# Two x blocks and the second-stage weights as float32 through the ScalarE and SyncE queues, in a convolution and spectral-mixing kernel

## The chip, the cores and the metric

The kernel runs on one core of a Trainium2 chip. The time is the device time of one execution in microseconds (us). The engines are TensorE (PE; its weight loads are PEld in the profile), VectorE (DVE), ScalarE (ACT), GpSimd (POOL) and SyncE (SP). Transfers can be issued from the queues of POOL, SP and ACT; the core has 16 DMA engines that serve them all.

## The reference

Two stages follow each other. The inputs are float32.

```python
# x: (8, 3264, 192), weight: (8 heads, 7 taps)
w = softmax(weight, axis=-1)
# causal convolution of 7 taps along the sequence; head h has channels 24*h .. 24*h+23
c[b, s, h, :] = sum_k w[h, k] * x_padded[b, s + k, h, :]      # 6 zero rows in front

X = rfft(c, axis=1)[:, :64]                                   # 64 modes, w_r and w_i: (64, 192, 192)
Yr = X.real @ w_r - X.imag @ w_i                              # per mode
Yi = X.real @ w_i + X.imag @ w_r
u = c + irfft(Yr + 1j*Yi, n=3264, axis=1)                     # all other modes are zero
out = u + relu(u @ w_ch)                                      # w_ch: (192, 192)
```

## The kernel before

**Data.** The whole of x is kept on chip as bf16 in `xall`. A sequence of 3264 rows is cut into two halves of 1632 rows, each of six blocks of 256 rows and a rest of 96 rows. Sequences go in pairs `q` (four of them). One "block half" is a block `b` of one half `h` for both sequences of a pair: 128 partitions times two runs of 384 elements. There are 48 of them; the list `halves` has them in the order in which they are wanted, the last pair and the last block first. `load_halves(n)` (L188) issues the next n on POOL's queue, whose transfers turn float32 into bf16 on the way. `load_rest` (L199) issues the four transfers of the rests.

**Order of the work.** The schedule is manual: each engine runs its instructions in the order in which the program issues them. At the start

- SP loads `weight` into `wraw`, copied to 128 partitions (a source list of `[14, 4], [0, 32], [1, 14]`);
- POOL issues one block half, writes three index tables (`cidx`, `sidx`, `midx`, L212 to L216), then issues nine more halves, the rests and the other halves, with a few small constants (`ident`, `order`, `perm`) between;
- VectorE and ScalarE make the softmax of the taps and from it the band matrices of the convolution (`band`; masks from `cidx` L228, softmax L232 to L248, taps put in place L253, copies of the band L256 to L264). VectorE then makes the phases of the Fourier tables from `sidx` and `midx` (L265 to L269), of which ScalarE takes the sines (`table(0)`, L277 to L279); VectorE clears some entries of that table (L282).

**Convolution and Fourier sums.** PE first does `rows_ahead` (L338), which needs the first two block halves and whose result ScalarE copies (L343), and then 24 filler matmuls (L524). Then come six units of two parts each, with eight heads in a unit; one head is 16 matmuls (L385) into one of four pairs of PSUM banks, which VectorE or ScalarE empties (L399, L401). The first unit reads ten block halves: eight of its own, and for the rows before them the two of the next block, which the matmuls with partitions 64 to 127 read a little later. VectorE adds and subtracts the halves (L419), PE makes the Fourier sums (`dft`, L436), and transposes (L493) fill in between.

**Mode weights.** `load_w` (L319) loads the weights of the modes in 16 groups on POOL's queue, after x and after the second-stage weights. PE multiplies them from L590 on, with the last transposes between. Some groups wait until a buffer is free (`wnext`).

**Second stage.** `wa` holds rows 0 to 127 of `w_ch`, `wb` the rows 128 to 191 twice, and `wc` (made from `wa` by ScalarE, L921) the two halves of `wa` swapped. They are needed from the mode stage on. The products are on L737, the clamp is on L783, the sum on L805 and the stores on SP's queue behind it.

The lines of the loads at the start that the change touches:

Of the kernel before, what the change touches and what calls it, by code (L numbers as in the profile page):

```python
# [12 lines left out]
F32 = mybir.dt.float32  # L13
BF16 = mybir.dt.bfloat16
# [5 lines left out]
def kernel(  # L20
# [9 lines left out]
    nc = tc.nc  # L30
    B, S, D = x.shape
# [8 lines left out]
    P = 128  # L40
    NQ = B // 2
    HS = S // 2
# [19 lines left out]
    def sb(name, shape, dtype):  # L62
        return pool.tile([P] + shape, dtype, tag=name, name=name)
# [8 lines left out]
    xall = sb("xall", [NQ, TQ, 2, D], BF16)  # L72
# [5 lines left out]
    mixa = sb("mixa", [3 * 2 * B * MODES], BF16)  # L78
    xt = mixa[:, :].rearrange("p (j k m) -> p j k m", j=3, k=2 * B)
    zw, zy = [mixa[:, B * D * t:B * D * (t + 1)].rearrange("p (b d) -> p b d", b=B) for t in range(2)]  # L80
    wa = sb("wa", [D], BF16)
    wb = sb("wb", [D], BF16)
    wc = sb("wc", [D], BF16)
    ident = sb("ident", [P], BF16)
    ascale = sb("ascale", [1], F32)
# [8 lines left out]
    spare = sb("spare", [NK - 4, 2 * D], F32)  # L94
# [13 lines left out]
    ctw = [ct[:, q, :, :, :].rearrange("p k t c -> p (k t c)") for q in range(NQ)]  # L108
# [76 lines left out]

    halves = [(q, b, h) for q in range(NQ)[::-1] for b in range(NBH)[::-1] for h in range(2)]

    def load_halves(n):  # L188
        for _ in range(n):
            q, b, h = halves.pop(0)  # L190
            k = 2 + 4 * b + 2 * h
            src = bass.AP(tensor=x.tensor, offset=x.offset + (2 * q * S + HS * h + 2 * P * b) * D,
                          ap=[[2 * D, P], [S * D, 2], [1, 2 * D]])
            nc.gpsimd.dma_start(out=xall[:, q, k:k + 2, :, :].rearrange("p k t d -> p k (t d)"), in_=src)  # L194


    R0 = (P - RR) // 2
# [1 line left out]
    def load_rest():  # L199
        for i in range(2):  # L200
            for h in range(2):
                src = bass.AP(tensor=x.tensor, offset=x.offset + (i * S + HS * (2 - h) - RR) * D,
                              ap=[[2 * D, RR // 2], [2 * S * D, NQ], [1, 2 * D]])
                nc.gpsimd.dma_start(out=xall[64 * h + R0:64 * h + 64, :, i, :, :].rearrange("p q t d -> p q (t d)"),
                                    in_=src)
# [2 lines left out]
    wr3 = wraw.rearrange("p (h k) -> p h k", h=G4)  # L208
    nc.sync.dma_start(out=wraw, in_=bass.AP(tensor=weight.tensor, offset=weight.offset,
                                            ap=[[G4 * KK, 4], [0, 32], [1, G4 * KK]]))  # L210
    load_halves(1)
    nc.gpsimd.iota(cidx, pattern=[[1, PW]], base=0, channel_multiplier=-1, allow_small_or_imprecise_dtypes=True)  # L212
    nc.gpsimd.iota(sidx.rearrange("p (b a) -> p b a", a=2), pattern=[[2 * P, NBH + 1], [1, 2]], base=0,
                   channel_multiplier=2, allow_small_or_imprecise_dtypes=True)
    nc.gpsimd.iota(midx.rearrange("p (r j) -> p r j", r=2), pattern=[[1, 2], [2, JH]], base=0,
                   channel_multiplier=0, allow_small_or_imprecise_dtypes=True)  # L216
    load_halves(9)
    load_rest()
    nc.vector.memset(packed, 0.0)
    nc.scalar.copy(out=bd3[:, :, PW:2 * PB], in_=packed[:, 0:1].unsqueeze(2).to_broadcast([P, H, 2 * PB - PW]))  # L220
# [13 lines left out]
                            in1=wmax.unsqueeze(2).to_broadcast([P, G4, KK]), op=ALU.subtract)  # L234
    nc.scalar.activation(out=wexp, in_=wsub, func=ACT.Exp)
    nc.scalar.activation(out=sgn[:], in_=halfpi[:], func=ACT.Sin)

    for h in range(2):
        rest = sidx[64 * h:64 * h + 64, 2 * NBH:NTF]
# [11 lines left out]
    for k in range(KK):  # L251
        e, v = divmod(KK - 1 - k, 2)
# [3 lines left out]
    for g in range(4):  # L256
        for r in range(4):
            c0 = 32 * (r % 2)
            dst = bd4[32 * r:32 * r + 32, G4 * g:G4 * (g + 1), :, c0:c0 + PW]
            srcv = pk4[32 * g:32 * g + 32, :, :, :]  # L260
            if r == 3 or (r == 2 and g > 1):
                nc.scalar.copy(out=dst, in_=srcv)
            else:
                nc.vector.tensor_copy(out=dst, in_=srcv)  # L264
    nc.vector.tensor_tensor(out=kp3, in0=sidx.unsqueeze(2).to_broadcast([P, NTF, MODES]),  # L265
                            in1=midx.unsqueeze(1).to_broadcast([P, NTF, MODES]), op=ALU.mult)
    nc.vector.tensor_scalar(out=turns, in0=kprod, scalar1=MAGIC, scalar2=None, op0=ALU.add)
# [20 lines left out]
    def select(dst, fill, base, pattern):  # L288
        nc.gpsimd.affine_select(out=dst, in_=dst, compare_op=ALU.not_equal, fill=fill, base=base,
                                pattern=pattern, channel_multiplier=1)  # L290

    load_halves(4)
    nc.gpsimd.memset(ident[:], 0.0)
    load_halves(2)
# [11 lines left out]
        load_halves(2)  # L306
        select(pv, 1.0 if c else -1.0, -JH * (1 - c), [[-1, JH], [-2 * JH, 2]])
    load_halves(len(halves))
    nc.gpsimd.dma_start(out=wa[:, :], in_=moe_w_ch[0:P, :])
    for i in range(2):  # L310
        nc.gpsimd.dma_start(out=wb[64 * i:64 * i + 64, :], in_=moe_w_ch[P:D, :])


    NG = MODES // 4
# [205 lines left out]

    rows_ahead(NQ - 1)

    for _ in range(24):
        nc.tensor.matmul(cz[3][64:P, 0, 0:2 * D], ahead[64:P, :], xall[64:P, NQ - 1, 2 + 4 * (NBH - 1), :, :].rearrange(  # L524
            "p t d -> p (t d)"), start=True, stop=True, tile_position=(64, 64), skip_group_check=True)
    prev = []
# [2 lines left out]
    for k, u in enumerate(units):  # L529
# [5 lines left out]
        for h in range(H):  # L535
            conv_head(u, h, "v" if h in ((0, 1, 3, 5) if k == 0 else (0, 4)) else "a")
            if h in (1, 5) and prev:
                q, b0, nb, rest = prev.pop(0)
# [383 lines left out]
    for g, beside in enumerate((0, 1, 1, 1, 2, 2, 2, 2, 2, 2, 2, 2, 2, 2, 0, 0)):  # L922
        d = g // 2
# [64 lines left out]
```

## Time and profile before

| | |
|---|---|
| median of 3 runs | 173.25 us (172.99 to 174.1) |
| profiled execution | 172.99 us |
| its span, from the first to the last instruction | 171.1 us |
| busy: PE, DVE, ACT, POOL | 92%, 73%, 72%, 38% of the span |
| POOL's queue | 23088 packets, 19.96 MB written |
| read from HBM, written to HBM | 39.43 MB, 20.45 MB |

The page divides the span into 40 equal slices; a digit is the busy share of an engine in tenths. In the rows of the timeline and of the groups stand the start in us, the duration in us, the engine, the line, the operation, out<-in with partitions x elements, and in brackets the idle time of the engine just before and what ended it. A list of waits has: who waited for whom, us in total, how often, the longest. In the view by stretches ("windows") each row has the stretch, its length, then the busy time and the number of instructions of PE, PEld, DVE, ACT and POOL, the granted TensorE clock, the mean load of the DMA engines (over 1 where packets overlap) and GB/s. In the view of DMA, a queue's row has packets, MB and the time its packets took as a share of 16 engines; the GB/s line has 40 slices of the stretch asked for; an issue's row has the number of transfers, KB of each, and us from issue to landing.

### The profile page before, as it was taken

Reading aid. Unit: us, or ns where it says so; the run is one execution under the profiler, and the core shown is the slowest. Engines: PE = TensorE matmul, PEld = TensorE weight load, DVE = VectorE, ACT = ScalarE, POOL = GpSimd, SP = SyncE. Lnnn points to the kernel's source line nnn. Section 1 sums busy time; section 2 is a strip of 40 time slices with the busy share of each in tenths; the row PEclk is TensorE's granted clock in tenths of the full one; section 3 lists DMA queues with packets and bytes.
Section 4 is the critical chain, followed back from the end, with each engine's and each line's share of the span. In section 5 each row is a group of like instructions: output and inputs, shape, how many; then the busy total and the mean of one; then the engine's idle time right before and its main releaser. Section 6 shows DMA issues by size and latency. Waiting matters only on the chain.

```text
span 171.1 us, 6152 instructions
## 1 busy us (share of the span) xinstructions
PE 157.1 (92%) x2599; PEld 118.9 (69%) x2599; DVE 125.3 (73%) x242; ACT 122.6 (72%) x224; POOL 64.4 (38%) x108
## 2 busy tenths in 40 slices
PE   0499999899999999998999999999999999999970
PEld 0255676566766666776776775888999989999930
DVE  3991857876493999944456562699989999899980
ACT  6656377858597688376685672779889899888840
POOL 7967999676766754434334002500000000000000
PEclk9999999999999999999999999999999999999995
DMA  2999999999999999999999993499969999899994
GB/s 28 162 183 200 201 201 204 198 201 201 203 204 194 201 209 203 206 206 206 206 207 207 206 179 71 108 387 340 322 244 390 371 361 374 318 357 377 353 382 144
DMA packets 38335, 40.71 MB, mean 238 GB/s; under 512 B 3652, under 2 KB 38212, under 8 KB 38308
## 3 DMA queue, kind: packets, MB, share of 16 engines
q0 software_dynamic: 23088, 19.96, 73.0%
q1 hardware_dynamic: 14948, 20.16, 32.7%
q8 instruction: 20, 0.33, 0.7%
q10 hardware_dynamic: 272, 0.20, 0.3%
q14 instruction: 7, 0.06, 0.1%
HBM read 39.43 MB, written 20.45 MB: 350 GB/s over the span
## 4 chain that ended last, share of the span: by engine, by line
PE 50%; DMA 34%; POOL 9%; issue 2%; DVE 1%; ACT 1%; POOLq 0%; DVEq 0%
DMA xall<-in_x_dram 23%; PE outleft L737 18%; PE mixright L737 16%; DMA ct<-in_moe_w_i_dram 11%; POOL xall L194 8%; PE trleft L493 7%; PE mixright L590 3%; PE trleft L737 2%; PE mixright L618 2%; DVE xall L805 1%; PE mixright L911 1%; PE mixright L640 1%; ACT wc L921 0%; POOL ct L323 0%; ACT band L601 0%
## 5 line engine op out<-in xcount | busy, mean ns | idle before, releaser
L737 PEld LDWEIGHTS <-ct 64*128 64x128 bf16 x624 | 41.0, 94 | 5.0 <-PE trleft L737 0.5
L737 PE MATMUL outleft<-mixa,gtab 64*128 64x384 bf16 x182 | 41.9, 323 | 0.1
L737 PE MATMUL mixright<-mixa,gtab 64*128 64x384 bf16 x182 | 41.0, 323 | 0.0
L194 POOL DMA_DIRECT2D xall<-in_x_dram x48 | 34.7, 734 | 8.6 <-DMA xall<-in_x_dram 7.5
L385 PEld LDWEIGHTS <-band 64*64 64x64 bf16 x768 | 24.8, 107 | 14.0 <-DMA xall<-in_x_dram 0.8
L737 PEld LDWEIGHTS <-gtab 64*128 64x128 bf16 x416 | 30.8, 94 | 2.8 <-PE outleft L737 1.1
L385 PE MATMUL cvleft<-xall,band 64*64 64x384 bf16 (+2 forms) x384 | 29.2, 341 | 0.1
L385 PE MATMUL cvright<-xall,band 64*64 64x384 bf16 (+2 forms) x384 | 28.8, 340 | 0.0
L783 ACT ACTIVATE outleft<-outleft 128x384 f32<-128x384 f32 x53 | 24.4, 476 | 4.6 <-PE outleft L737 2.3
L783 ACT ACTIVATE mixright<-mixright 128x384 f32<-128x384 f32 x51 | 23.7, 478 | 3.2 <-PE mixright L737 1.0
L737 PE MATMUL outleft<-wb,ct 64*128 64x192 bf16 x104 | 23.1, 243 | 0.0
L737 PE MATMUL outleft<-wa,ct 64*128 64x192 bf16 x104 | 22.9, 243 | 0.0
L737 PE MATMUL outleft<-wc,ct 64*128 64x192 bf16 x104 | 21.7, 243 | 0.0
L401 ACT CAST xall<-cvleft 128x864 bf16<-128x864 f32 (+1 forms) x20 | 16.3, 859 | 7.1 <-PE cvleft L385 4.9
L493 PEld LDWEIGHTS <-xall 128*128 128x128 bf16 x312 | 17.6, 98 | 4.7 <-issue 1.6
L737 PE MATMUL mixright<-wa,ct 64*128 64x192 bf16 x84 | 19.5, 243 | 0.0
L737 PE MATMUL mixright<-wb,ct 64*128 64x192 bf16 x84 | 19.3, 243 | 0.0
L466 DVE COPY ct<-trleft 128x1024 bf16<-128x1024 bf16 (+1 forms) x18 | 11.8, 668 | 10.0 <-PE trleft L493 9.0
L737 PE MATMUL mixright<-wc,ct 64*128 64x192 bf16 x84 | 17.9, 243 | 0.0
L805 DVE TENSOR_TENSOR arena<-outleft,xall 128x384 f32<-128x384 f32 x27 | 14.4, 553 | 2.5 <-PE outleft L737 2.3
L493 PE MATMUL trleft<-ident,xall 128*128 128x128 bf16 x234 | 16.0, 220 | 0.0
L401 ACT CAST xall<-cvright 128x864 bf16<-128x864 f32 (+1 forms) x14 | 11.9, 866 | 5.6 <-PE cvleft L385 3.1
(149 smaller groups left out, 287.0 us busy)
## 6 DMA issues: line engine op xcount, KB each, us to landing
xall<-in_x_dram POOLq DMA_DIRECT2D x48, 192.0 KB, 7.5
out_dram<-arena SPq DMA_DIRECT2D x23, 384.0 KB, 3.8
out_dram<-xall SPq DMA_DIRECT2D x13, 384.0 KB, 4.1
out_dram<-ct SPq DMA_DIRECT2D x8, 384.0 KB, 3.9
ct<-in_moe_w_r_dram POOLq DMA_DIRECT2D x10, 288.0 KB, 10.5
ct<-in_moe_w_i_dram POOLq DMA_DIRECT2D x10, 288.0 KB, 10.9
arena<-in_moe_w_r_dram POOLq DMA_DIRECT2D x6, 288.0 KB, 11.4
arena<-in_moe_w_i_dram POOLq DMA_DIRECT2D x6, 288.0 KB, 11.6
```

The source lines that it names most:

```text
L194: nc.gpsimd.dma_start(out=xall[:, q, k:k + 2, :, :].rearrange("p k t d -> p k (t d)"), in_=src)
L385: return nc.tensor.matmul(o, bd3[r, h, base:base + 64], mv, start=start, stop=stop, tile_position=(64 * src, 64 * dst), skip_group_check=True)
L401: nc.scalar.copy(out=dst, in_=srcv)
L466: nc.vector.tensor_copy(out=out, in_=in_)
L493: nc.tensor.transpose(o, cv.rearrange("p i d -> p (i d)")[:, P * blk:P * blk + P], ident[:])
L590: nc.tensor.matmul(yp[32 * p4:32 * p4 + 2 * B, :], xt[:, j, :, m], wbuf(g)[:, p4, j, :], start=(j == 0), stop=(j == 2), tile_position=(0, ...
L618: nc.tensor.transpose(ets[t][:, g, :], yall[:, md(d), g, 64 * t:64 * t + P], ident[:])
L640: nc.tensor.matmul(o, yet[:, k, b, modes], w[:], start=(k == 0), stop=(k == 1), skip_group_check=True)
L737: m = nc.tensor.matmul((Z[s % NZ] if bank is None else bank)[:, cols], l, r, start=start, stop=stop, skip_group_check=True)
L783: act = nc.scalar.activation(out=z, in_=z, func=ACT.Relu)
L805: add = nc.vector.tensor_tensor(out=o[:, :, a, :], in0=Z[s % NZ][:, 0:2 * D].rearrange("p (i d) -> p i d", i=2), in1=c_rows(q, kk)[:, a, : ...
L911: nc.tensor.matmul(sums[bank][:, 0:2 * D], ident[:], call[:, 0, 0, 0, :, :], start=True, stop=True, skip_group_check=True)
```

## The change

- Two block halves, the seventh and eighth of the list, are loaded as float32 to a place in `ct` that is free at that time: one by ScalarE's queue, as that engine's first instruction, one by SP's queue behind `weight`. ScalarE casts them into `xall` after the softmax's exponential and the loading of the sine function.
- `w_ch` comes as float32 through SP's queue into `spare`, in two transfers: rows 0 to 127, and rows 128 to 191 twice with one source list that begins with `[0, 2]`. ScalarE casts both at once into `wab`, of which `wa` and `wb` are now parts, after its copies of the band. The three transfers of POOL for `wa` and `wb`, between x and the mode weights, are gone.
- POOL issues three block halves ahead of the index tables, then six more; so nine go ahead of the rests, and with the two early ones eleven of the list.
- 18 filler matmuls in place of 24.

```diff
-    wa = sb("wa", [D], BF16)
-    wb = sb("wb", [D], BF16)
+    wab = sb("wab", [2 * D], BF16)
+    wa, wb = wab[:, 0:D], wab[:, D:2 * D]
...
+    def next_half(n=0):
+        q, b, h = halves.pop(n)
+        k = 2 + 4 * b + 2 * h
+        return (xall[:, q, k:k + 2, :, :].rearrange("p k t d -> p k (t d)"),
+                bass.AP(tensor=x.tensor, offset=x.offset + (2 * q * S + HS * h + 2 * P * b) * D,
+                        ap=[[2 * D, P], [S * D, 2], [1, 2 * D]]))
+
     def load_halves(n):
         for _ in range(n):
-            q, b, h = halves.pop(0)
-            k = 2 + 4 * b + 2 * h
-            src = bass.AP(tensor=x.tensor, offset=x.offset + (2 * q * S + HS * h + 2 * P * b) * D,
-                          ap=[[2 * D, P], [S * D, 2], [1, 2 * D]])
-            nc.gpsimd.dma_start(out=xall[:, q, k:k + 2, :, :].rearrange("p k t d -> p k (t d)"), in_=src)
+            dst, src = next_half()
+            nc.gpsimd.dma_start(out=dst, in_=src)
+
+    early = []
+    for i in range(2):
+        dst, src = next_half(6)
+        stage = ctw[0][:, 8 * D * i:8 * D * i + 8 * D].bitcast(F32).rearrange("p (k e) -> p k e", k=2)
+        early.append((dst, stage, src))
+    nc.scalar.dma_start(out=early[0][1], in_=early[0][2])
...
-    load_halves(1)
+    nc.sync.dma_start(out=early[1][1], in_=early[1][2])
+
+    nc.sync.dma_start(out=spare[:, 0, 0:D], in_=moe_w_ch[0:P, :])
+    nc.sync.dma_start(out=spare[:, 0, D:2 * D], in_=bass.AP(tensor=moe_w_ch.tensor, offset=moe_w_ch.offset + P * D,
+                                                            ap=[[0, 2], [D, 64], [1, D]]))
+    load_halves(3)
     nc.gpsimd.iota(cidx, ...)
     nc.gpsimd.iota(sidx, ...)
     nc.gpsimd.iota(midx, ...)
-    load_halves(9)
+    load_halves(6)
     load_rest()
...
     nc.scalar.activation(out=sgn[:], in_=halfpi[:], func=ACT.Sin)
+    for dst, stage, _ in early:
+        nc.scalar.copy(out=dst, in_=stage)
...
                 nc.vector.tensor_copy(out=dst, in_=srcv)
+    nc.scalar.copy(out=wab[:], in_=spare[:, 0, :])
     nc.vector.tensor_tensor(out=kp3, ...)
...
     load_halves(len(halves))
-    nc.gpsimd.dma_start(out=wa[:, :], in_=moe_w_ch[0:P, :])
-    for i in range(2):
-        nc.gpsimd.dma_start(out=wb[64 * i:64 * i + 64, :], in_=moe_w_ch[P:D, :])
...
-    for _ in range(24):
+    for _ in range(18):
         nc.tensor.matmul(cz[3][64:P, 0, 0:2 * D], ahead[64:P, :], ...)
```

## The prediction

> **What bounds the kernel now.** First the page: its share line of TensorE (PE), its DMA line, and the chain of waits.
>
> ```profile
> span 171.1 us, 6152 instructions
> ...
> PE   0499999899999999998999999999999999999970
> ...
> DMA  2999999999999999999999993499969999899994
> ...
> DMA xall<-in_x_dram 23%; PE outleft L737 18%; PE mixright L737 16%; DMA ct<-in_moe_w_i_dram 11%; POOL xall L194 8%; PE trleft L493 7%; PE mixright L590 3%; PE trleft L737 2%; PE mixright L618 2%; DVE xall L805 1%; PE mixright L911 1%; PE mixright L640 1%; ACT wc L921 0%; POOL ct L323 0%; ACT band L601 0%
> ```
>
> Two resources run side by side: the DMA engines are full from about 4 to 101 us, and PE is full from the second slice on. The chain goes through DMA until 77 us, but a chain shows one path. So I looked at PE's own waits: the weight-load rows of the timeline, then the list of waits of PE from 12 to 110 us.
>
> ```profile
> 15.85 5.44 PEld L385 LDWEIGHTS <-band 64*64 64x64 bf16 x115 [0.44 <-DMA xall<-in_x_dram]
> ...
> 21.92 0.45 PEld L493 LDWEIGHTS <-xall 128*128 128x128 bf16 x8 [0.30 <-issue]
> ...
> 26.63 0.51 PEld L385 LDWEIGHTS <-band 64*64 64x64 bf16 x15 [0.35 <-DMA xall<-in_x_dram]
> ...
> 101.81 0.26 PEld L590 LDWEIGHTS <-mixa 128*16 128x16 bf16 x12 [0.32 <-DMA arena<-in_moe_w_i_dram]
> ```
>
> ```profile
> PE cvleft L493 <- ACT xall L401: 0.5, 1, 0.5
> PE mixright L618 <- ACT band L601: 0.5, 1, 0.5
> PE cvright L493 <- ACT xall L401: 0.4, 1, 0.4
> PE mixright L580 <- ACT mixa L457: 0.2, 1, 0.2
> ```
>
> PE waits for x twice (until 15.85, when the tenth half is in, and until 26.63) and once for mode weights (101.81). Between, it waits 1.6 us in all, never for a transfer. So the transfers set when the convolution gets going; from 26.6 us PE has no slack, and every delay at 26.6 goes through to the end, save the 0.32 us at 101.8. What the change is worth is decided before 27 us.
>
> **The change, part by part: the transfers.** Rows of the DMA view: the GB/s line of 0 to 5 us (40 slices), stretches of the windows, a steady stretch (20 to 30 us), the weight's transfer (0 to 5 us, and 2 to 3.5 us) and the one that ScalarE's queue issues near the end (165 to 171 us).
>
> ```profile
> GB/s 0 0 0 0 0 0 0 0 0 0 0 0 0 0 0 0 0 3 6 6 6 6 24 34 20 16 27 45 33 45 111 141 215 203 203 203 172 142 141 178
> ```
>
> ```profile
> 4.00:5.00 1.00, 0.00 (x0) 0.00 (x0) 0.72 (x4) 0.34 (x2) 1.00 (x3) 1.00 1.21 182
> 5.00:6.00 1.00, 0.48 (x1) 0.12 (x1) 0.84 (x6) 1.00 (x1) 1.00 (x2) 1.00 0.99 147
> 6.00:7.00 1.00, 0.03 (x2) 0.03 (x2) 0.99 (x7) 0.36 (x2) 1.00 (x3) 1.00 0.98 137
> ...
> 9.00:10.00 1.00, 1.00 (x5) 0.56 (x4) 0.92 (x4) 0.98 (x3) 1.00 (x3) 1.00 1.18 159
> ```
>
> ```profile
> q0 software_dynamic: 2743, 1.98, 130.0%
> ```
>
> ```profile
> q1 hardware_dynamic: 132, 0.01, 1.4%
> ...
> arena<-in_weight_dram SPq DMA_DIRECT2D x1, 7.0 KB
> ```
>
> ```profile
> q1 hardware_dynamic: 104, 0.01, 3.5%
> ```
>
> ```profile
> q10 hardware_dynamic: 272, 0.20, 9.8%
> ```
>
> ```profile
> xall<-in_x_dram POOLq DMA_DIRECT2D x48, 192.0 KB, 7.5
> ```
>
> (The last row is the page's list of issues.) POOL's queue writes 1.98 MB in 10 us (twice that is read, since it turns float32 into bf16), so a half of 192 KB takes 0.99 us, a sixteenth on each engine, and with 7.5 us from issue to landing about eight are out. Full rate begins at slice 31 of 40, 3.9 us. Before that the engines are idle, and in 5 to 7 us they lose (198 - 147) + (198 - 137) = 112 KB, 0.57 us: the second half is issued late, behind the three index tables. With 16 KB in 4 to 5 us and some 83 KB in 7 to 11 us (39 of them in 9 to 10) the shortage is 1.07 us. Check: 3.9 + 10 x 0.99 + 1.07 = 14.9 us for the tenth half, and PE goes on at 15.85: 0.95 us for landing.
>
> ```profile
> 0.74 0.72 SPq L209 DMA_DIRECT2D arena<-in_weight_dram  x1
> ...
> 1.27 0.87 POOL L194 DMA_DIRECT2D xall<-in_x_dram  x1 [0.82 <-POOLq L972]
> ...
> 2.23 0.19 POOL L212 IOTA arena<- 128x36 f32 x1
> ...
> 2.65 6.51 POOL L194 DMA_DIRECT2D xall<-in_x_dram  x9
> ...
> 50.31 0.56 POOL L309 DMA_DIRECT2D wa<-in_moe_w_ch_dram  x1 [0.24 <-DMA xall<-in_x_dram]
> ```
>
> After the change ScalarE's queue and SyncE's issue from 0.74 us at 0.72 us each, and move from slice 17, 2.2 us. The idle front is filled and the gap of 5 to 7 us is covered. Taken off POOL's queue are two halves (1.98 us) and wa and wb (96 KB, 0.5 us). Added in front are the same halves, which read as much and so take 0.99 us each, and w_ch twice 96 KB.
>
> The point is the shape of the last of these: its source list begins with [0, 2]. The weight's begins with [.., 4], and its 128 runs come with 4 further packets (132); the store on ScalarE's queue, whose list begins with 128, has 256 runs and 16 closing ones (272). I read it as four engines and sixteen. So the load of wb would run on two, 64 packets of 768 B on each. The store's 768 B packets took 9.8% of 16 x 6 us over 272, 35 ns each. Work on those two engines until POOL's eighth half is through (the tenth of before): 2.2 start + 32 weight packets 1.1 + two halves 1.98 + wa 8 x 0.035 = 0.28 + wb 64 x 0.035 = 2.24 + eight halves 7.92 + the shortage of 7 to 11 us 0.42 = 16.1 us, against 14.9. The x stream is **1.2 us later**, though the other engines are ahead: a half is there when its slowest engine is done, and POOL issues the next one only when an old one has landed (the releaser in the row at 50.31 below), so the lead stays unused. Bounds: if the weight's packets cost nothing and no shortage stays, 14.6 (-0.3); if all of it stays, 16.8 (+1.9).
>
> The Trainium skill, "DMA: Bandwidth & Descriptors", section "Why a DMA increments its semaphore by 16 and not by 1", says that the number of engines is the largest up to 16 that divides the outermost dimension of both sides; the 4 and 16 closing packets agree. By it wb gets two engines; without it, the sum is that of the second rival.
>
> **ScalarE, VectorE and the banks.** Timeline rows:
>
> ```profile
> 4.23 0.17 DVE L232 TENSOR_REDUCE arena<-arena 128x2 f32<-128x14 f32 x1 [0.60 <-DMA arena<-in_weight_dram]
> 6.17 0.20 ACT L236 ACTIVATE sgn<-halfpi 128x1 f32<-128x1 f32 x1
> 7.20 1.96 ACT L262 COPY band<-arena 32x144 bf16<-32x144 bf16 x6 [0.82 <-DVE arena L253]
> 7.30 6.92 PE L524 MATMUL cvright<-xall,ahead 64*64 64x384 bf16 x21
> 9.16 1.59 ACT L343 CAST xall<-cvleft 16x768 bf16<-16x768 f32 x2
> 13.31 0.95 ACT L277 ACTIVATE ftab<-arena 128x896 bf16<-128x896 f32 x1 [2.55 <-DVE ascale L270]
> 15.13 1.04 ACT L279 ACTIVATE ftab<-arena,halfpi 128x896 bf16<-128x896 f32 x1
> 16.25 0.39 DVE L282 MEMSET ftab<- 16x128 uint32 x2 [2.84 <-DMA xall<-in_x_dram]
> 17.38 0.96 DVE L399 CAST xall<-cvleft 128x768 bf16<-128x768 f32 x1 [0.73 <-PE cvright L385]
> 18.78 0.80 ACT L401 CAST xall<-cvright 128x768 bf16<-128x768 f32 x1 [2.61 <-PE cvleft L385]
> 19.43 0.96 DVE L399 CAST xall<-cvleft 128x768 bf16<-128x768 f32 x1 [0.23 <-PE cvleft L385]
> 73.46 0.48 ACT L438 CAST loose<-cvright 128x384 bf16<-128x384 f32 x1 [0.33 <-PE cvright L436]
> ```
>
> The index tables come behind two more issues of 0.72 us, 1.4 us later. VectorE had 0.60 us of wait for the weight, so it is 0.8 us late if the weight lands as before, up to 2.0 if that is delayed by sharing engines; I take 1.1, so the table's input, which released ScalarE at 13.31, is there at 14.4.
>
> ScalarE gets two casts of a half (768 elements; nearest row 0.80) and the cast of wa and wb (384 elements; 0.48). Before the table of sines it had 2.55 us of wait, which would hide them. But the last cast waits for wb. Nothing of x between: 2.2 + 1.1 + 0.99 + 0.99 + 0.28 + 2.24 = 7.8, landed 8.8. With an x packet (0.99/16 = 0.062 us) after each of 98 packets that SyncE's queue still has from 3.9 us on (10 of the weight, 16, 8 and 64): 13.9, landed 14.9. I take 14, because the weight's packets, alone at 6 GB/s, slow down once x flows: 104 are through by 3.5 us, 132 by 5. Behind that cast stand the two casts of L343, the table, and, on VectorE, the clearing L282 (the view names a DMA; but it clears entries that L279 writes, and starts 0.08 us after that ends) with the first head's eviction behind it. So ScalarE: sgn until 7.5, halves until 9.1, band until 11.0, wb at 14, cast 14.5, L343 16.1, table (13.31 to 16.17, 2.86) 19.0, L282 19.4. The eviction of head 0 can start at 19.4 instead of 17.38, and ends at 20.4. Head 4 needs that bank: it began at about 19.4 (head 3 done) and now, x being 1.2 late, at 20.6. The delay is just covered by x's; if wb is 0.7 us later still, it isn't.
>
> Six of the 24 filler matmuls go, 0.33 us each (6.92 for 21); they lie under the wait for x, worth nothing. The band copies, before the table's input on VectorE and at 11.0 on ScalarE, are in ahead of x, whose sixth half of POOL lands at 16.1 - 2 x 0.99 + 0.95 = 15.1.
>
> **Sum.** Unit 0 and the wait at 26.63: +1.2. At 101.8 the weights' stream is 1.2 - 0.5 = 0.7 late, PE 1.2: its wait of 0.3 goes. Total **+0.9 us**. The profiled execution took 172.99 (1.9 around the span), so 173.9; it lies 0.26 below the median of the three runs, on which I put the forecast: **174.2**. A measurement of this kernel tells about 1%, 1.7 us, from no change: slower is above 175.0, faster below 171.5.
>
> **Rivals.** *wb holds ScalarE* (0.2): x late by 1.9 and wb in at 15.5. The table ends at 20.5, L282 at 20.9, head 0 is out at 21.9, and head 4 starts 2.5 late. Less the 0.35 us at 26.63 and the 0.3 at the end: +1.9, 175.1. For it: three in-order steps stand behind one cast; against: ScalarE had 2.55 + 2.61 us to spare.
>
> *wb is spread over the engines* (0.2), the other side: 8 packets instead of 64 give 14.2 us on the engines that carry the weight, 0.7 earlier (up to 1.8 if that costs nothing). Table from 14.4 to 17.3, L282 until 17.7, head 4 from 18.7: no obstacle until x is 0.7 early. So -0.7, and the wait at 101.8 goes: -1.0, 172.2. It decides when the two engines' load falls under 14.9 - 13.9 = 1.0 us of wb, some 29 packets. Against it: the 132.
>
> *The whole front is won* (0.05): 2 us earlier all along, 171.3; VectorE's 0.8 us late tables speak against it. The remaining 0.07 is for mishaps beyond the bounds, mostly slower.
>
> **How the numbers follow.** The forecast has 0.48 (own range 173.1 to 175.3). The range 172.0 to 176.0 takes in the second rival's value and the first's with the late end of x, and leaves out some 0.15. Faster: the third rival and a tail of the second, 0.08. Slower: over half of the first, a fifth of the forecast's, the rest's, and some for late copies that I bounded only by rows of other shapes: 0.36. Same: 0.56.
>
> **What would show it.** Right: 130 closing and data packets for wb; the first conv stretch of PE ending its wait near 17 us, L277 near 16, PE's wait at 26.6 moved to near 27.8, none at the last mode weights. Wrong: conv under way before 15 us; the cast of wa and wb on ScalarE starting by 11; POOL's last x issue before 49.35.

## The result, and the profile after

The changed kernel takes 175.53 us (median of 5, 175.05 to 176.83) against 173.25 us (172.74 to 174.1) on the same chip: a ratio of 1.0137, 95% interval 1.0096 to 1.0178. It is slower by 1.0 to 1.8%, 2.3 us by the medians.

The profiled execution of it took 176.83 us, the longest of the five. A second profile, taken of the same kernel (e10 below), took 174.93 and lies nearer the median, so sizes are given from both. Line numbers after the change are some 17 higher: L385 has become L402, L493 L510, L282 L302, L343 L360, L399 L416, L401 L418, L524 L541, L590 L607, L194 L198.

First the page after: share line of PE, DMA line, and the chain of waits by engine.

```profile
span 175.0 us, 6146 instructions
...
PE   0079899989999999998999999999999999999970
...
DMA  7799999999999999999999962379969999999994
...
PE 81%; DMA 6%; ACT 4%; POOL 3%; DVE 2%; issue 1%; POOLq 0%; DVEq 0%; ACTq 0%
```

The DMA engines are busy from the first slice (7 instead of 2), as the change means it; but PE's third slice, full before (9), is a 7. The span is 3.9 us longer. The rows of PE's weight loads show where:

```profile
18.31 7.13 PEld L402 LDWEIGHTS <-band 64*64 64x64 bf16 x115 [0.90 <-DMA xall<-in_x_dram]
...
30.39 0.56 PEld L402 LDWEIGHTS <-band 64*64 64x64 bf16 x16 [0.17 <-issue]
...
105.67 0.26 PEld L607 LDWEIGHTS <-mixa 128*16 128x16 bf16 x12 [0.32 <-issue]
```

The same rows of the second profile:

```profile
17.68 3.46 PEld L402 LDWEIGHTS <-band 64*64 64x64 bf16 x50 [0.80 <-DMA xall<-in_x_dram]
...
29.23 1.87 PEld L402 LDWEIGHTS <-band 64*64 64x64 bf16 x42 [0.17 <-issue]
```

Before, PE went on at 15.85 us and, for the second unit, at 26.63. Now the first is 18.31 (17.68 in the second profile), 1.8 to 2.5 us late, and the other 30.39 (29.23), 2.6 to 3.8 late. PE keeps that delay to the end: its last group of matmuls (L754) starts at 168.24 us (167.09), the same group before (L737) at 164.38, 3.9 (2.7) us earlier. So what came to pass ahead of 31 us is the whole of it. Nothing is won back at the wait of 101.81: the row at 105.67 has the same 0.32 us of idle time, only no transfer is named for it any more. The spans grew by 3.9 and 2.1 us, and not by 3.9 and 2.7, because the end of the work varies too: from the issue of the last store to the end of the span 4.25 to 5.9 us pass in the fourteen profiles of this case.

What DMA did in the first 15 us, packets by queue; q0 is POOL's queue, q1 SyncE's, q10 ScalarE's:

```profile
q0 software_dynamic: 2083, 1.51, 66.5%
q1 hardware_dynamic: 678, 0.60, 23.7%
q10 hardware_dynamic: 272, 0.39, 9.6%
```

Of SyncE's 678 packets 132 are the weight's, 272 the half's (as many as ScalarE's half has) and 144 those of `wa` (128 and 16). 130 are left for `wb`: 128 and 2.

The view of DMA from 0 to 5 us, and from 3.75 to 5.25:

```profile
GB/s 0 0 0 0 0 0 0 0 0 0 0 0 0 0 61 147 111 98 37 160 369 393 406 393 393 381 274 193 112 51 24 7 2 1 1 2 1 0 1 2
```

```profile
DMA packets 52, 0.01 MB, mean 4 GB/s; under 512 B 49, under 2 KB 52, under 8 KB 52
...
q0 software_dynamic: 2, 0.00, 9.0%
q1 hardware_dynamic: 50, 0.00, 2.0%
```

At 2.4 to 3.4 us ScalarE's float32 half moves, at up to 406 GB/s, and lands at 3.9. (SyncE's queue has moved only 0.06 MB by 5 us; its half lands at 7.7.) Then for 1.5 us next to nothing moves: 52 packets, 49 of them small ones. Nothing in the forecast had such a standstill.

Timeline rows of ScalarE, VectorE and PE:

```profile
6.27 0.17 DVE L249 TENSOR_REDUCE arena<-arena 128x2 f32<-128x14 f32 x1 [1.21 <-DMA arena<-in_weight_dram]
8.87 0.48 PE L355 MATMUL cvleft<-xall,ahead 64*64 64x384 bf16 x1 [8.87 <-DMA xall<-in_x_dram]
15.00 0.51 ACT L284 CAST wab<-spare 128x384 bf16<-128x384 f32 x1 [3.15 <-DMA spare<-in_moe_w_ch_dram]
15.52 1.59 ACT L360 CAST xall<-cvleft 16x768 bf16<-16x768 f32 x2
17.02 0.94 ACT L297 ACTIVATE ftab<-arena 128x896 bf16<-128x896 f32 x1
19.96 0.39 DVE L302 MEMSET ftab<- 16x128 uint32 x2 [5.10 <-ACT ftab L299]
20.38 0.96 DVE L416 CAST xall<-cvleft 128x768 bf16<-128x768 f32 x1
```

ScalarE does wait 3.15 us for `wb`, and the sine table, VectorE's clearing and head 0's eviction follow one behind the other, as forecast. So four suspects stand in one trace: `wb` on two engines, the standstill, ScalarE's wait, and the clock, of which more below.

### The profile page after: what moved, and what is told of

Read it like the earlier page. It is cut to its first block, busy times and chain, and to the rows that moved or that the text cites. A ratio compares the mean times of both kernels' runs of the same rounds, so it can differ in the third digit from the quotient of the medians.

```text
span 175.0 us, 6146 instructions
## 1 busy us (share of the span) xinstructions
PE 157.1 (90%) x2593; PEld 118.9 (68%) x2593; DVE 124.7 (71%) x242; ACT 124.4 (71%) x227; POOL 61.0 (35%) x103
## 4 chain that ended last, share of the span: by engine, by line
PE 81%; DMA 6%; ACT 4%; POOL 3%; DVE 2%; issue 1%; POOLq 0%; DVEq 0%; ACTq 0%
PE outleft L754 18%; PE mixright L754 16%; PE cvright L402 11%; PE cvleft L402 11%; PE trleft L510 7%; DMA xall<-in_x_dram 6%; PE cvright L453 4%; PE mixright L607 3%; POOL xall L198 3%; PE trleft L754 2%; ACT xall L418 2%; PE mixright L635 2%; PE cvleft L510 1%; PE cvleft L453 1%; DVE xall L822 1%
## 5 line engine op out<-in xcount | busy, mean ns | idle before, releaser
L754 PEld LDWEIGHTS <-ct 64*128 64x128 bf16 x624 | 41.0, 94 | 4.9 <-PE trleft L754 0.5
L754 PE MATMUL outleft<-mixa,gtab 64*128 64x384 bf16 x182 | 41.9, 322 | 0.1
L754 PE MATMUL mixright<-mixa,gtab 64*128 64x384 bf16 x182 | 41.0, 323 | 0.0
L198 POOL DMA_DIRECT2D xall<-in_x_dram x46 | 33.2, 729 | 9.3 <-DMA xall<-in_x_dram 7.4
L402 PEld LDWEIGHTS <-band 64*64 64x64 bf16 x768 | 25.8, 111 | 14.8 <-DMA xall<-in_x_dram 0.9
L754 PE MATMUL outleft<-wab,ct 64*128 64x192 bf16 x208 | 34.6, 243 | 0.0
L754 PEld LDWEIGHTS <-gtab 64*128 64x128 bf16 x416 | 30.8, 94 | 3.0 <-PE outleft L754 1.1
L402 PE MATMUL cvleft<-xall,band 64*64 64x384 bf16 (+2 forms) x384 | 29.9, 353 | 0.5 <-DMA xall<-in_x_dram 0.5
L402 PE MATMUL cvright<-xall,band 64*64 64x384 bf16 (+2 forms) x384 | 30.1, 350 | 0.0
L754 PE MATMUL mixright<-wab,ct 64*128 64x192 bf16 x168 | 29.9, 243 | 0.0
L754 PE MATMUL outleft<-wc,ct 64*128 64x192 bf16 x104 | 21.7, 243 | 0.0
L418 ACT CAST xall<-cvleft 128x864 bf16<-128x864 f32 (+1 forms) x20 | 16.3, 859 | 7.4 <-PE cvleft L402 3.0
L510 PEld LDWEIGHTS <-xall 128*128 128x128 bf16 x312 | 17.6, 98 | 4.7 <-issue 1.6
L754 PE MATMUL mixright<-wc,ct 64*128 64x192 bf16 x84 | 17.8, 243 | 0.0
L510 PE MATMUL trleft<-ident,xall 128*128 128x128 bf16 x234 | 16.0, 220 | 0.0
L418 ACT CAST xall<-cvright 128x864 bf16<-128x864 f32 (+1 forms) x14 | 11.9, 866 | 5.5 <-PE cvleft L402 3.0
L481 ACT COPY ct<-trleft 128x1024 bf16<-128x1024 bf16 x12 | 12.2, 1013 | 3.0 <-PE trleft L510 2.8
L416 DVE CAST xall<-cvright 128x864 bf16<-128x864 f32 (+1 forms) x10 | 10.2, 1016 | 2.4 <-DMA xall<-in_x_dram 0.8
```

The source lines that it names most:

```text
L198: nc.gpsimd.dma_start(out=dst, in_=src)
L402: return nc.tensor.matmul(o, bd3[r, h, base:base + 64], mv, start=start, stop=stop, tile_position=(64 * src, 64 * dst), skip_group_check=True)
L481: nc.scalar.copy(out=out, in_=in_)
L510: nc.tensor.transpose(o, cv.rearrange("p i d -> p (i d)")[:, P * blk:P * blk + P], ident[:])
L754: m = nc.tensor.matmul((Z[s % NZ] if bank is None else bank)[:, cols], l, r, start=start, stop=stop, skip_group_check=True)
```

## Experiments

"Before" and "after" name the two kernels. Each ratio is to before on the same chip; the medians of before were 173.23 us (e1 to e4), 173.65 (e5 to e8) and 173.3 (e9 to e12).

### e1: `wb` by sixteen engines

```diff
-    nc.sync.dma_start(out=spare[:, 0, D:2 * D], in_=bass.AP(..., ap=[[0, 2], [D, 64], [1, D]]))
+    for i in range(2):
+        nc.sync.dma_start(out=spare[64 * i:64 * i + 64, 0, D:2 * D], in_=moe_w_ch[P:D, :])
```

> Changed kernel, but rows 128 to 191 of w_ch come in two transfers of 64 rows each (source and target lists begin with 64), so 4 packets of 768 B on each of 16 engines instead of 64 on each of two. Theory A (the load on two engines delays x there and holds ScalarE's cast): the cast of wa and wb starts by 12 us instead of 15.0, the clearing of the sine table near 18 instead of 19.96, the first unit's wait for x ends about 2 us earlier than the 18.31 of the changed kernel, and the time falls by 1.5 to 2.2 us, to about 173.5. Theory B (the float32 halves ahead of everything hold up the weight and POOL's first transfer): the first products of L355 stay near 8.9 us, and the time falls by less than 0.7 us, to 174.9 or more.

Measured: 174.63 us, ratio 1.0079 (1.0057 to 1.0101). DMA view of 0 to 15 us, and PE's and ScalarE's rows:

```profile
q1 hardware_dynamic: 708, 0.60, 23.2%
```

```profile
11.95 0.51 ACT L284 CAST wab<-spare 128x384 bf16<-128x384 f32 x1
...
16.61 5.44 PEld L402 LDWEIGHTS <-band 64*64 64x64 bf16 x116 [0.77 <-ACT arena L298]
...
27.01 4.00 PEld L402 LDWEIGHTS <-band 64*64 64x64 bf16 x88 [0.17 <-DMA xall<-in_x_dram]
```

708 packets, 160 for `wb` (two transfers of 64 and 16). The cast of `wab` starts at 11.95 with no wait, and PE goes on at 16.61 instead of 17.7 to 18.3. (It no longer waits for x by then: the row names ScalarE, and POOL's eighth half, the last that the first unit needs, was issued at 6.94 us and landed 9.1 us later, at 16.0.) So two engines it was, and that is worth 0.4 to 0.6 of the 1.2 to 1.4 per cent of loss; some 0.8 are left. The profiled execution here took 173.58 us, the fastest of its seven, and its rows show only +0.4 at the second unit (27.01 for 26.63) and +0.9 at PE's last group of matmuls (165.32 for 164.38), so they do not account for all of the 1.4 us that the median is above before.

### e2 and e3: the change in halves

e2 is after without its treatment of `w_ch`: the two transfers on SyncE's queue and the cast are gone, and POOL loads `wa` and `wb` behind x, as before.

```diff
-    nc.sync.dma_start(out=spare[:, 0, 0:D], in_=moe_w_ch[0:P, :])
-    nc.sync.dma_start(out=spare[:, 0, D:2 * D], in_=bass.AP(..., ap=[[0, 2], [D, 64], [1, D]]))
-    nc.scalar.copy(out=wab[:], in_=spare[:, 0, :])
...
+    nc.gpsimd.dma_start(out=wa, in_=moe_w_ch[0:P, :])
+    for i in range(2):
+        nc.gpsimd.dma_start(out=wb[64 * i:64 * i + 64, :], in_=moe_w_ch[P:D, :])
```

> Changed kernel, but wa and wb come through POOL's queue at the end of x as in the kernel before; the early float32 halves, the order of the index tables and the 18 fillers stay. Theory A: no two-engine load is left, so most of the loss goes: about 173.3. Theory B: the halves are still in front, PE's first products stay near 8.9 us, and the time stays at 174.9 to 175.5.

e3 keeps `w_ch` on SyncE's queue and drops the two early halves: POOL loads them in their turn.

```diff
-    nc.scalar.dma_start(out=early[0][1], in_=early[0][2])
-    nc.sync.dma_start(out=early[1][1], in_=early[1][2])
-    load_halves(6)
+    load_halves(7)
-    for dst, stage, _ in early:
-        nc.scalar.copy(out=dst, in_=stage)
```

> Changed kernel without the two early float32 halves and their casts: they come through POOL in the list's order; w_ch still through SyncE with the list that begins with 2. Theory A: the cast of wa and wb on ScalarE still waits until 12 to 14 us and x is still 2 us late on two engines; the time stays at 174.8 to 175.8. Theory B: POOL's first half lands near 5.2 us as before, PE's first products are near 5.5 us, and the time falls to about 173.6.

Measured: e2 173.21 us, ratio 0.9992 (0.997 to 1.0013); e3 175.63, ratio 1.0140 (1.0114 to 1.0167). The loss is wholly that of `w_ch`; the early halves are worth nothing that the times can tell, with it or without. PE's rows of e2, its DMA line of 0 to 15 us with POOL's row, then PE's rows of e3:

```profile
15.72 2.92 PEld L401 LDWEIGHTS <-band 64*64 64x64 bf16 x51 [0.77 <-issue]
...
26.80 4.28 PEld L401 LDWEIGHTS <-band 64*64 64x64 bf16 x94 [0.17 <-DMA xall<-in_x_dram]
```

```profile
GB/s 0 0 0 0 16 57 147 348 386 206 43 2 2 1 30 263 379 309 219 199 199 205 199 197 203 199 207 197 203 203 197 199 203 199 207 197 203 203 197 199
...
q0 software_dynamic: 2326, 1.69, 73.5%
```

```profile
18.17 6.30 PEld L393 LDWEIGHTS <-band 64*64 64x64 bf16 x115 [0.80 <-DMA xall<-in_x_dram]
...
28.75 2.32 PEld L393 LDWEIGHTS <-band 64*64 64x64 bf16 x47 [0.16 <-issue]
```

From before to e2 PE's start moves by -0.13 us (15.85, 15.72). But the row of e2 says issue and not DMA, so it does not tell when x was in. The transfers do. The first unit needs ten halves; the last of them is the tenth of POOL's queue before, and the eighth in e2. Issue and us from issue to landing, before:

```profile
8.37 0.79 POOL L194 DMA_DIRECT2D xall<-in_x_dram  x1
```

```profile
xall<-in_x_dram POOLq DMA_DIRECT2D x1, 192.0 KB, 7.4
```

The same in e2, and the last filler of PE there:

```profile
6.96 0.76 POOL L198 DMA_DIRECT2D xall<-in_x_dram  x1
```

```profile
xall<-in_x_dram POOLq DMA_DIRECT2D x1, 192.0 KB, 8.1
```

```profile
15.09 0.52 PE L540 MATMUL cvright<-xall,ahead 64*64 64x384 bf16 x1
```

So x for the first unit is in at 15.8 us before and at 15.1 in e2, 0.7 earlier. (In e7 below, whose loads are those of before, it is in at 15.5: two executions differ by some 0.3.) PE goes on at 15.72 all the same, since POOL's own second half, which `rows_ahead` needs, lands at 9.3 us instead of 6.9, and the fillers behind it run until 15.6. With `w_ch` in front, x for the first unit is in 2.3 us later than before (e3: 18.1) and 2.5 to 3.2 later than in e2 (after: 17.6 in e10, and 18.3).

At the second unit nothing of e2's lead is left. That unit needs the eighteenth half of the list, for which PE waits until 26.63 before: it lands, read in the same way, at 26.6 us before, at 27.0 in e2 and at 27.0 in e7. Over all fourteen profiles it lands at 26.3 to 27.2 us in the eight without `wb` on two engines, and at 28.4 to 29.0 in the six with it. This is the delay that the times show.

And e2 has the standstill too: the slices from 4.1 to 5.3 us have 2, 2 and 1 GB/s.

### e4: the index tables behind the third half, alone

```diff
-    load_halves(1)
+    load_halves(3)
...
-    load_halves(9)
+    load_halves(7)
```

(On the kernel before.)

> Kernel before with only the index tables moved behind the third block half of POOL. Theory A: harmless, since POOL's gap at 5 to 7 us closes and VectorE has slack: 173.0 (-0.3 to +0.1). Theory C (the late index tables make the band and the sine table late, and that costs): sine table 0.8 us later, time +0.5 to +0.8 us, 173.9.

Measured: 173.02 us, ratio 0.9993 (0.997 to 1.0015). VectorE's delay has cover; this edit is harmless. Its x for the first unit is in at 14.8 us, 1.0 earlier than before, and its eighteenth half at 26.3, 0.3 earlier.

### e5: the cast of `wab` behind the sine table

The line `nc.scalar.copy(out=wab[:], in_=spare[:, 0, :])` of after moves from ahead of `rows_ahead` to behind `table(0)`.

> Changed kernel with ScalarE's cast of wa and wb placed behind the three sine-table instructions instead of ahead of them. Theory A1 (the load on two engines costs by making x late): ScalarE's table starts near 14.7 us instead of 17.0, the first unit's wait for x still ends near 18.3, and the time stays within 0.5 us of the changed kernel, 175.0 to 175.6. Theory A2 (it costs by holding ScalarE): the first eviction starts 2 us earlier and the time falls by 1 to 2 us, to 174 or less.

Measured: 175.38 us, ratio 1.0113 (1.0076 to 1.0151). ScalarE's and PE's rows:

```profile
14.19 0.95 ACT L296 ACTIVATE ftab<-arena 128x896 bf16<-128x896 f32 x1 [1.06 <-DVE ascale L289]
...
16.96 0.49 ACT L548 CAST wab<-spare 128x384 bf16<-128x384 f32 x1
```

```profile
17.73 6.16 PEld L401 LDWEIGHTS <-band 64*64 64x64 bf16 x119 [0.84 <-DMA xall<-in_x_dram]
...
28.51 2.39 PEld L401 LDWEIGHTS <-band 64*64 64x64 bf16 x56 [0.17 <-issue]
```

The table starts at 14.19 instead of 17.02, nothing waits for `wb`, and the time is that of after within its interval. So ScalarE's wait is real and is not the main cost. e3 agrees: there the cast starts at 11.13 us and the table at 13.87, and the time is that of after. That the wait costs nothing is not shown. In after, e10 and e6, which have it, PE comes to the second unit 0.8 to 1.4 us behind x (in after at 30.39, the eighteenth half in at 29.0); in e5 and in e9 below it comes with x (28.51 and 29.04). The medians of e5 and after lie closer together than that, but their intervals are too wide to exclude it.

### e6, e7, e9: the clock

In after, the convolution runs at half rate for long. Groups of L402 from 18.3 to 23 us, then from 23.6 to 25.6 (mean ns of one behind the comma):

```profile
L402 PE MATMUL cvright<-xall,band 64*64 64x384 bf16 x32 | 4.0, 523 | 0.0
...
L402 PE MATMUL cvright<-xall,band 64*64 64x384 bf16 x32 | 2.1, 323 | 0.0
```

Full rate came at 23.4 us (20.8 in e10), in before at 17.4; unit 0 lasts 7.5 us (7.0) instead of 5.8. The fillers of both kernels use one 64x64 quarter of the array. So 30 groups of four, one on each quarter, took their place: in after (e6), in before (e7), and in e5's kernel (e9).

```diff
-    for _ in range(18):          # 24 in before
-        nc.tensor.matmul(cz[3][64:P, 0, 0:2 * D], ahead[64:P, :], ..., tile_position=(64, 64), ...)
+    for _ in range(30):
+        for r in (64, 0):
+            for c in (64, 0):
+                nc.tensor.matmul(cz[3][c:c + 64, r // 64, 0:2 * D], ahead[r:r + 64, :],
+                                 ..., tile_position=(r, c), ...)
```

> Changed kernel, fillers exchanged: 30 groups of four matmuls that fill all four quarters of the array, instead of 18 on one quarter. Theory D (part of the loss is PE's clock: fillers on one quarter leave it at half rate, so the first unit runs at half rate until 23.4 us): conv matmuls take 0.32 to 0.36 us from the start instead of 0.53, the first unit is shorter by about 1.5 us, time 174.0. Without D: no change, 175.5, or later by up to 2 us if the longer fillers delay the first head.

> Kernel before with the same 30 groups of four fillers. Theory D: the first unit, at half rate from 13.9 to 17.4 us before, runs at full rate; as x ends its wait at 15.85 only 0.6 to 0.8 us can be gained, and the wait for x at 26.6 (0.35 us) takes part of it back: 172.8 (-0.2 to -0.6). Without D: 173.2, or later if the fillers run past 15.85.

> Changed kernel with both covers off at once: the cast of wa and wb behind the sine table (as in the run before) and the 30 groups of fillers that keep PE's clock up. Theory F (three causes lie over each other: x late, ScalarE held, PE at half rate; each of the last two alone is hidden by the other): now the first unit is limited by x alone; it ends its wait near 17.8, ends near 23.2 us, unit 1 flows from 27.8, and the time is 174.5 to 174.8, better than either alone. Rival G (x alone decides, the others are worth nothing): no better than the late cast alone, 175.3.

Measured: e6 176.25 us, ratio 1.0151 (1.0113 to 1.0189); e7 173.65, ratio 1.0013 (0.999 to 1.0036); e9 174.99, ratio 1.0104 (1.0059 to 1.0149). The fillers by line, each with its shortest, median and longest in ns and its first and last start, of before, after, e6 and e7:

```profile
L524 PE MATMUL cvright<-xall,ahead x24: 524/524/524, 7.3 to 14.7; 64*64 64x384 bf16 x24
```

```profile
L541 PE MATMUL cvright<-xall,ahead x18: 524/524/524, 10.8 to 16.2; 64*64 64x384 bf16 x18
```

```profile
L543 PE MATMUL cvright<-xall,ahead x120: 322/323/525, 10.1 to 16.4; 64*64 64x384 bf16 x120
```

```profile
L526 PE MATMUL cvright<-xall,ahead x120: 322/323/526, 7.2 to 13.7; 64*64 64x384 bf16 x120
```

On one quarter every filler takes 524 ns for 5 to 7 us on end, and one starts 0.32 us after the other; on all quarters they turn to 323 ns on the way, with a group every 0.16 us, and the convolution is at full rate from its start. But no time comes of it. PE's rows of e7, the list of PE's first waits of e6 after its wait for x, and PE's rows of e9:

```profile
25.09 0.74 PEld L385 LDWEIGHTS <-band 64*64 64x64 bf16 x9 [0.41 <-issue]
27.01 4.04 PEld L385 LDWEIGHTS <-band 64*64 64x64 bf16 x93 [1.17 <-DMA xall<-in_x_dram]
```

```profile
PE cvleft L402 <- DVE xall L416: 1.4, 1, 1.4
```

```profile
28.38 0.10 PEld L401 LDWEIGHTS <-band 64*64 64x64 bf16 x1 [0.17 <-DMA xall<-in_x_dram]
29.04 1.97 PEld L401 LDWEIGHTS <-band 64*64 64x64 bf16 x47 [0.56 <-DMA xall<-in_x_dram]
```

In e7 the first unit is done sooner, and PE waits 1.17 us for x at the second, until 27.01. In e6 a faster PE runs into the banks that ScalarE's wait keeps full (1.4 us for VectorE's eviction). In e9 both are gone, and PE still stands until 29.04 for x: 2.4 us later than the 26.63 of before. So the second unit's x is late by itself, and this alone makes PE some 2 us late: its last group of matmuls starts 2.4 us after that of before in e9, and 2.0 in e5. What half rate and full banks add to it is not settled: 174.99 lies between the 174.8 of theory F and the 175.3 of rival G and decides neither. (e9's profiled execution took 176.08, above its median.)

### e8 and e11: the weight by sixteen engines

The weight's source list begins with 4, and its packets are the small ones of the standstill. e8 is e2 with the weight in four transfers whose lists begin with 32; e11 is before, with the tables as in e4 and the same four.

```diff
+    for g in range(4):
+        nc.sync.dma_start(out=wraw[32 * g:32 * g + 32, :],
+                          in_=bass.AP(tensor=weight.tensor, offset=weight.offset + g * G4 * KK,
+                                      ap=[[0, 32], [1, G4 * KK]]))
```

> The changed kernel with wa and wb on POOL's queue (e2), and weight loaded in four transfers of 32 partitions whose source lists begin with 32, so 8 packets of 56 B on each engine instead of 32 on each of four. Theory E (while the weight's small packets run, from 3.25 to 5.9 us, all other packets stand still): the standstill from 3.75 to 5.25 us goes, POOL's first packets flow 1 to 1.5 us earlier than the 6.26 us of e2, the first unit ends its wait 1 us earlier, and the time falls to 172.5. Without E (the standstill has another cause): POOL's first packets stay near 6.3 us, time 173.2.

> Kernel before with the index tables behind the third block half and weight in four transfers of 32 partitions, no float32 halves, w_ch on POOL's queue. Theory E (weight's packets on four engines hold up x): x flows at full rate from 3.2 us instead of 4, unit 1's wait for x ends near 25.6 instead of 26.4, time 172.4 (-0.6 to -0.9 against the kernel before). Otherwise 173.1, as with the tables alone.

Measured: e8 174.05 us, ratio 1.0021 (0.9994 to 1.0049); e11 173.86, ratio 1.0029 (0.9994 to 1.0063). DMA from 3.75 to 5.25 us in e8, and its row of PE:

```profile
DMA packets 295, 0.19 MB, mean 123 GB/s; under 512 B 70, under 2 KB 295, under 8 KB 295
```

```profile
16.05 2.45 PEld L403 LDWEIGHTS <-band 64*64 64x64 bf16 x51 [0.77 <-issue]
```

The standstill is gone (123 GB/s for 12 in e2), which fits the reading that the weight's packets on four engines went with it. Yet PE goes on at 16.05, not earlier than e2's 15.72, and x for the first unit is not there earlier either: at 15.7 us in e8 (15.1 in e2) and at 15.7 in e11 (14.8 in e4). The three more issues on SyncE's queue also put its float32 half later in e8: issued at 2.55 us instead of 1.52, there at 9.8 instead of 7.3. The expectation of a gain fell, for e11 too.

### e10 and e12: after once more, and all at once

e10 is after unchanged, for a second profile beside others. e12 is e11 with 26 groups of fillers on all quarters in place of the 24.

> The changed kernel as it is, once more, beside the run before it on the same chip. All theories: 175.5, with the wait for x ending near 18.0 to 18.3, and the time at which PE's matmuls of 64x384 fall from 0.53 to 0.36 us somewhere between 19.5 and 23.5, as its profile of 176.83 was the longest of five.

> The same with 26 groups of four fillers that keep PE's clock up. If x comes earlier (theory E) the half clock is the next thing in the way: another 0.3 to 0.5 us, 172.0. If x does not come earlier: no gain over the run before it, 173 to 173.6.

Measured: e10 175.26 us, ratio 1.0118 (1.0076 to 1.0160), which with the first 1.0137 puts after at 2.0 to 2.4 us over before. e12 174.67, ratio 1.0077 (1.0045 to 1.0108): slower than before, though each of its parts alone made no difference that can be told. One of its rows of PE:

```profile
27.12 5.14 PEld L387 LDWEIGHTS <-band 64*64 64x64 bf16 x115 [0.78 <-DMA xall<-in_x_dram]
```

It waits for x at the second unit until 27.12, 0.5 late. Its profiled span is 1.8 us longer than that of before: PE's last group of matmuls starts 0.8 late (165.22), and 1.0 us more passes behind the issue of the last store (5.9 us for 4.95), a part that varies from execution to execution. So the 1.4 us of its median stay open in part. No version tried beats before.

## Why the forecast was right or wrong

The forecast was 174.2 us, with 173.1 to 175.3 as its own range and 172.0 to 176.0 with the rivals; it gave 0.56 to no change that can be told and 0.36 to slower, above 175.0. The measured 175.53 (175.26 in e10) lies in the wide range and above 175.0: the less likely of the two came. It lies inside because the rivals had widened the range; the sum itself was 1.1 to 1.4 us short of the 2.0 to 2.3 measured.

**Right: `wb` on two engines.** 130 packets, and e1 recovers part of the loss. The Trainium skill's rule ("DMA: Bandwidth & Descriptors", "Why a DMA increments its semaphore by 16 and not by 1") agrees with that count, and with the 160 of e1.

**Right: the price of `w_ch` in front.** The sum had 0.28 us for `wa` and 2.24 for `wb`, 2.5 in all. Measured at x for the first unit: 2.3 (before to e3) and 2.5 to 3.2 (e2 to after).

**Wrong: the credit for the front.** This is the step that failed: "The idle front is filled and the gap of 5 to 7 us is covered", with engines at work from 2.2 us. It turned 2.5 into 1.2, a gain of 1.3 us. e2, which has the early halves and the later tables and nothing of `w_ch` in front, shows what it was worth: x for the first unit is in 0.7 us earlier (0.4 against e7), PE's start 0.13 earlier, the second unit's x no earlier, and the time the same. e4 has 1.0 us at the first unit from the later tables alone, so the early halves added nothing to it that shows. The bytes agree. Up to 15 us before had 2.03 MB of x through POOL's queue; e2 has 1.69 and, as float32, two halves of 0.39 MB, which are 0.39 MB as bf16: 2.08 in all, a quarter of one half ahead. What was filled at 2.4 to 3.4 us was lost at 3.75 to 5.25. With the credit struck out, the sum is +2.5 at the first wait for x, or 175.8 us. Measured are +1.8 (e10) and +2.5 at the first unit's x, +1.8 and +2.4 at the second's, and +2.0 to 2.3 in the medians. The bound of +1.9 that the forecast gave for x was too low, since it let the old shortage stay but not the late start: the engines were still to be at work from 2.2 us on.

**Right in time, wrong in reason: the fillers.** "Worth nothing": e6 and e7 bear that out. But the forecast took PE's rate for given. Half rate held on 6 us longer than before (3.4 in e10) and made unit 0, together with the banks that ScalarE's wait kept full, longer by 1.2 to 1.7 us, so the mark "near 27.8" for the second unit was missed twice over (29.23 and 30.39). x alone would have missed it: the eighteenth half landed at 28.4 and 29.0. Nor do the fillers always lie under the wait for x: in e2, where x is earlier, they are what holds PE until 15.6.

**Right: the queue on ScalarE and VectorE.** Forecast and measured: cast of `wab` 14 and 15.00, L360's casts 14.5 and 15.52, sine table 16 and 17.02, clearing 19.4 at its end and 20.35. All are about 1 us late, since `wb` was there at 15.0: the forecast's own working had 14.9 as the late end and took 14. That the delay is covered by x was said; the times of e3 and e5 agree with it as far as their intervals reach, while the traces leave 0.8 to 1.4 us at the second unit open.

**Wrong: the wait at 101.8.** The sum took 0.3 off for it. It is gone by name only: the same 0.32 us of idle time stands at 105.67, with no transfer to wait for, and PE is 3.9 us late ahead of it and behind it. The term was worth nothing.

**Right: the tables.** e4 and e2 cost nothing.

**The rivals.** "`wb` holds ScalarE" gave 175.1, nearest to the measured time, but by another road: its x, late by 1.9, came true, while e5 takes ScalarE's wait away and stays at 1.0113. "`wb` is spread" gave -1.0 us; e1 makes it so and is at +1.4: the credit for the front again, and 0.2 MB more in front of x, which is in 0.2 us later than before at the first unit where the rival had 0.7 earlier. "The whole front is won" fell with e2. The marks of a wrong forecast (convolution before 15 us, the cast by 11, POOL's last x issue before 49.35) all stayed away; the last was at 51.1 us.

**Open.** Why flow without the standstill (e8, e11) brings x no earlier; where the lead that e2 and e4 have at the first unit's x goes before the second's; what makes up e1's 1.4 us beyond the 0.4 to 0.9 us of its rows; how much of after's loss is ScalarE's wait and half rate; and part of e12.

## What to carry to other kernels

A transfer that is wanted late does not belong ahead of a stream that is waited for, however idle the queue there looks; and where its outermost source dimension is small, price it on the few engines that carry it, for everything behind it waits for the slowest of them. A gain by "filling an idle front" is to be proved in bytes of the awaited tensor through by a fixed time, and by when its transfers land: the time at which an engine goes on tells it only where the engine was still waiting for them. Before a wait on PE is mended, look at what is late next: here the clock, ScalarE's banks and the second unit's x lay within 1.5 us of each other.

## What the runs showed of the hardware that was not expected

- A float32 half from ScalarE's queue, with a little of SyncE's beside it, moved at up to 406 GB/s for a microsecond; then, for 1.5 us, 4 GB/s, while packets of the weight (56 B of source each) were under way on four engines. With the weight on sixteen engines 123 GB/s flowed at that place.
- A queue with little to move is slow beside a full one: from 9 to 14.25 us SyncE's queue got 105 packets through, some 53 on each engine if they are `wb`'s on two, while POOL's got 1381, 86 for each of sixteen. That fits packets of the two queues taking turns on those two engines.
- Back-to-back matmuls on one 64x64 quarter of the array stayed at 524 ns for 7.4 us (24 of 24 in before); on four quarters they went to 323 ns after 2.6 us in e6 (30 of 120 slow), 2.8 in e7 and 5.5 in e9. The view by stretches shows a granted clock of 1.00 all the while, so half rate is read from the matmuls alone (524 against 323 ns, and starts 0.32 against 0.16 us apart). The Trainium skill ("TensorE: Matmul & The Clock Gate", "Part 1: The HAM clock gate") has half rate end after a busy window of about 3.4 us; the groups of four lie on both sides of that, the quarter-array rows do not agree, and the measurement decides.

The row of that view for 11 to 16 us of after, with the granted clock behind the engines:

```profile
11.00:16.00 5.00, 5.00 (x19) 2.68 (x16) 3.61 (x9) 1.81 (x5) 1.96 (x4) 1.00 1.31 204
```
